# Top-k attention with an MLP on one core: values of the first 14 units half a step later, reciprocals one round later, three hurried pairs instead of five, eight pairs of q and k on chip instead of five

## The chip, the core and the metric

The kernel runs on one core of a Trainium2 chip. Its time is device microseconds (us), the median of several runs. One further execution was taken with the hardware profiler on; the views of the profile below come from that one.

## What is computed

Attention with a top-32 mask over 8 x 8 heads of 576 positions and 64 dimensions, and then a two-layer MLP with a leaky ReLU over the 4608 tokens:

```
scores = scale * q @ k^T                   # per head, 576 x 576
kth    = 32nd largest score of each row
scores = where(scores >= kth, scores, -1e9)
attn   = exp(scores - max); attn /= (sum(attn) + 1e-9)
x      = (attn @ v), heads side by side    # 4608 x 512
out    = leaky(x @ w_in) @ w_out           # 512 -> 2048 -> 512, slope 0.01
```

## The kernel before, in words

**Units and steps.** Two heads make a pair (32 pairs; four pairs are one batch element). A *unit* is 128 query rows of both heads of a pair, or the last 64 rows of two pairs. There are 144 units, 18 for each batch element. The main loop has one *step* s for each unit, and step s works on four units at once: the top-k of unit s, the mask and the exponents of unit s-1, the normalizing and the transposing of unit s-2, and the scores of units s+2 and s+3 (in even steps).

**What a unit passes through.** Scores: TensorE (PE) multiplies q and k into PSUM (L210), ScalarE (ACT) copies them to SBUF (L217). Top-k: VectorE (DVE) finds 32 maxima in four *rounds* of eight (L240, L245, L248). Mask: GpSimd (POOL; L258, L259). Exponents with row sums: ACT (L262), then `ze`, the sums plus 1e-9 (L267). Reciprocal of `ze`: DVE (L271). Normalizing: ACT (L274). Transposing: ACT splits the 32-bit weights into two 16-bit halves (L283), two DMAs write them to DRAM (`apart`, L284), and a DMA transpose reads them back as `wT` (L286), all DMAs issued in program order by SyncE (SP). Values: PE multiplies `wT` with v (`weigh_values`, L323), and ACT copies the product into x (`keep_values`, L337). When the four pairs of 128 or 256 tokens have their x, the MLP of this *chunk* can start.

**Hurried pairs.** An odd unit n in `HURRIED` (L425) is transposed by PE (L296) and copied by ACT (L302) instead of going through DRAM, and the values of units n-1 and n are then due one step sooner. `values_at` (L427) says in which step values are due; before, they are placed at the end of that step.

**Order of the work.** The order is written out by hand in the loop over s; every engine keeps it. A step has seven calls of `mlp_steps` between the four DVE rounds; each puts a share of MLP work into PE's order. The share is `EARLY_SHARE` (530) while chunk 2 is not yet ready; afterwards `slot_budget` spreads what is ready evenly up to the step in which the next chunk becomes ready. Chunks 0 and 1 have 128 tokens (units 0 to 3 and 4 to 7), all later ones 256; chunk 2 is units 8 to 15.

**Buffers.** `LOADED` = 5 pairs of q and k are in SBUF at a time. `load_more` (called at the end of each step) loads pair p when the scores of the last unit of pair p-5 are issued. The pool `raws` holds the weights as they arrive from DRAM (three tiles of 8 KB in each partition, tag `raw`); they are used only while the weights are rounded, ahead of the main loop. Further: five buffers `s_sb`, three `wT`, two `split`, in PSUM two `wide` and one `narrow`.

Of the kernel before, what the change touches and what calls it, by code (L numbers as in the profile page):

```python
# [8 lines left out]
F32 = mybir.dt.float32  # L9
U32 = mybir.dt.uint32  # L10
U16 = mybir.dt.uint16
# [8 lines left out]
def kernel(  # L20
# [14 lines left out]
    NPAIR, P, S = qT.shape  # L35
# [14 lines left out]
    WCH = 1024  # L50
# [5 lines left out]
    LOADED, LOADED_V = 5, 5  # L56
# [3 lines left out]
    loads = ctx.enter_context(tc.tile_pool(name="loads", bufs=LOADED))  # L60
    raws = ctx.enter_context(tc.tile_pool(name="raws", bufs=3))
# [33 lines left out]
    def load_weights(n):  # L95
        if n >= NPIECE:
            return
        if not AS_WORDS:
            nc.sync.dma_start(piece(n), weights[n])
            return  # L100
        raw_of[n] = raws.tile([P, WCH, 4], U16, name="raw")
        nc.sync.dma_start(raw_of[n].rearrange("p n w -> p (n w)"), weights[n])
# [50 lines left out]
    qk_of, v_of = {}, {}  # L153

    def load_qk(pi):
        qt = loads.tile([P, S], F32, name="qt")
        kt = loads.tile([P, S], F32, name="kt")
        nc.sync.dma_start(qt, qT[pi])
        nc.sync.dma_start(kt, kT[pi])
        qk_of[pi] = qt, kt  # L160

    def load_v(pi):
        v_of[pi] = loads.tile([P, NKC, 2, D], F32, name="vt", bufs=LOADED_V)
        nc.sync.dma_start(v_of[pi], vk[pi])
# [104 lines left out]
    def reciprocals(u):  # L269
        u.rz = small.tile([P, 2], F32, name="rz")  # L270
        nc.vector.reciprocal(u.rz, u.ze)  # L271

    def normalize(u, i):
        nc.scalar.activation(u.s[i], u.s[i], AF.Copy, bias=0.0, scale=u.rz[:, i:i + 1])  # L274
# [33 lines left out]
    def x_at(token):  # L308

        c = 0  # L310
        while token >= CHUNKS[c]:
            token -= CHUNKS[c]
            c += 1
        return c, token
# [47 lines left out]
    def mlp(ch):  # L362

        n = CHUNKS[ch]
        t0 = sum(CHUNKS[:ch])
        x = x_of[ch]
        if ch < EARLY:
            yield from hidden_of_few(x)
        for f0 in range(0, NFC if ch >= EARLY else 0, 2):
            ph = ps_ml.tile([P, 2, CHMAX], F32, name="ph", tag="ml")  # L370
            for i in range(2):
                f = f0 + i
                for c in range(HP):
                    nc.tensor.matmul(  # L374
                        ph[:, i, 0:n], w_in[c][:, f * P:(f + 1) * P], x[c][:, 0:n],
                        start=(c == 0), stop=(c == HP - 1),
                    )
                    if c == 1 or i == 0 and c == HP - 1:
                        yield 2 * max(n, 225)
            nc.scalar.activation(gT[:, f0:f0 + 2, 0:n], ph[:, :, 0:n], AF.Prelu, alpha=SLOPE)  # L380
            yield 2 * max(n, 225)
        for r0 in range(0, n, P):
            m = min(P, n - r0)
            pz = ps_ml.tile([P, 512], F32, name="pz", tag="ml")
            for f in range(NFC):
                nc.tensor.matmul(  # L386
                    pz[0:m, 0:DMODEL], gT[:, f, r0:r0 + m], w_out[f // 4][:, f % 4, :],
                    start=(f == 0), stop=(f == NFC - 1),
                )
                if f % 2 and f + 1 < NFC:  # L390
                    yield 2 * DMODEL
            o_sb = work.tile([P, DMODEL], F32, name="o_sb", bufs=1)
            nc.scalar.copy(o_sb[0:m], pz[0:m, 0:DMODEL])
            nc.sync.dma_start(out[t0 + r0:t0 + r0 + m, :], o_sb[0:m])
            yield 2 * DMODEL

    def mlp_cost(ch):
        n = CHUNKS[ch]
        if ch < EARLY:
            return NFC * DMODEL + NFC // 4 * (HP * 512 + 2 * P)  # L400
        return NFC * HP * max(n, 225) + -(-n // P) * NFC * DMODEL
# [4 lines left out]
    def mlp_steps(budget):  # L406
        owed[0] += budget
        while owed[0] > 0:
            if running[0] is None:
                if not ready:  # L410
                    owed[0] = 0.0
                    return
                running[0] = mlp(ready.pop(0))
            cost = next(running[0], None)
            if cost is None:
                running[0] = None
            else:
                owed[0] -= cost
                backlog[0] -= cost
# [2 lines left out]

    LAG = 3
    HURRY = 20
    HURRIED = {3, 7, 15, 23, 31}  # L425

    def values_at(n):  # L427

        return n + LAG + (n + LAG) % 2 - ((n | 1) in HURRIED)

    steps = units

# [3 lines left out]
    done_tokens, ready_at = [0] * len(CHUNKS), []  # L436
    for n, u in enumerate(steps):
        ch, _ = x_at(u.b * S + u.q0)
# [2 lines left out]
            ready_at.append((values_at(n), ch))  # L441
    assert [ch for _, ch in ready_at] == list(range(len(CHUNKS)))

    def attended(s):
        for at, ch in ready_at:
            if at == s:
                ready.append(ch)
                backlog[0] += mlp_cost(ch)

    def slot_budget(s):  # L450

        after = [at for at, _ in ready_at if at >= s]
        until = after[0] if after else s
        if len(after) >= len(CHUNKS) - EARLY:
            return EARLY_SHARE
        return backlog[0] / ((until + 1 - s) * SLOTS)

    EARLY_SHARE = 530
    SLOTS = 7

    with tc.manual_schedule():
        last = {p: n for n, u in enumerate(steps) for p in u.pairs}

        def load_more(s):

            for of, load, n, lag in ((qk_of, load_qk, LOADED, -2), (v_of, load_v, LOADED_V, LAG + 1)):
                while len(of) < NPAIR and (len(of) < n or last[len(of) - n] + lag <= s):
                    load(len(of))


        for n in range(3):
            load_weights(n)
        rounding = {}
        for n in range(NPIECE + 2):
            for i in (n, n - 1, n - 2) if AS_WORDS else ():
                if 0 <= i < NPIECE:
                    if i == n:
                        rounding[i] = round_weights(i)
                    next(rounding[i], None)
            load_weights(n + 3)  # L480
            if 6 <= n < 6 + HP:
                load_qk(n - 6)
            elif n == NPIECE - 3:
                first_scores(steps[0])
            elif n == NPIECE:
                first_scores(steps[1])
            if n == NPIECE - 1:
                load_v(0)
                load_v(1)

        def values(s):
            due = [u for n, u in enumerate(steps) if values_at(n) == s]
            if due:
                po = ps_sc.tile([P, 2, 512], F32, name="wide", bufs=2)[:, 0, 0:2 * P]
                po = po.rearrange("p (u n) -> p u n", u=2)
            else:
                return
            for part in (weigh_values, keep_values):
                for n, u in enumerate(due):
                    part(u, po[:, n, :])  # L500
            attended(s)

        for s in range(len(steps) + LAG + 1):
            cur, old, older, new = unit(s), unit(s - 1), unit(s - 2), ()
            if s % 2 == 0:
                new = [u for u in steps[s + 2:s + 4] if u]
            picks = top_k(cur) if cur else iter(())
            budget = slot_budget(s)

            def slot():  # L510
                next(picks, None)

            slot()
            if old:
                mask(old, 0)
                mask(old, 1)
            if older:
                reciprocals(older)
                normalize(older, 0)
                normalize(older, 1)  # L520
            mlp_steps(budget)
            slot()
            if s - 2 in HURRIED:
                transpose_in_haste(older)
            mlp_steps(budget)
            if old:
                exponents(old, 0)
            if older:
                keep_transposed(older) if s - 2 in HURRIED else transpose(older)
            slot()  # L530
            mlp_steps(budget)
            mlp_steps(budget)
            slot()
            mlp_steps(budget)
            if old:
                exponents(old, 1)
                sums(old)
            if new and s < HURRY:
                scores(new)
            values(s)  # L540
            if new and s >= HURRY:
                scores(new)
            budget = slot_budget(s + 1)
            mlp_steps(budget)
            mlp_steps(budget)
            load_more(s)
        mlp_steps(1e9)

# [57 lines left out]
```

## Time and profile before

| | |
|---|---|
| median of 4 runs | 1491.6 us (1489.47 to 1492.33) |
| the profiled execution, its own time | 1488.68 us |
| span from its first to its last instruction | 1486.9 us |
| PE busy | 1397.9 us (94%) |
| DVE busy | 1328.6 us (89%) |
| ACT busy | 1094.7 us (74%) |
| POOL busy | 1096.1 us (74%) |
| mean granted PE clock | 0.980 |

How to read it: the span begins with the rounding of the weights (to about 68 us), then the 144 steps follow, and after about 1400 us only the MLP of the last chunks is left. "PEclk" in a table of windows is the granted clock of TensorE as a share of full speed. In a timeline a line gives start, duration, engine, line of the kernel, operation, tiles and count, and in brackets the idle time of the engine ahead of it with what ended it. One fp32 matmul of the program shows as two in the profile.

### The profile page before, as it was taken

Reading aid. Unit: us, or ns where it says so; the run is one execution under the profiler, and the core shown is the slowest. Engines: PE = TensorE matmul, PEld = TensorE weight load, DVE = VectorE, ACT = ScalarE, POOL = GpSimd, SP = SyncE. Lnnn points to the kernel's source line nnn. Section 1 sums busy time; section 2 is a strip of 40 time slices with the busy share of each in tenths; the row PEclk is TensorE's granted clock in tenths of the full one; section 3 lists DMA queues with packets and bytes.
Section 4 is the critical chain, followed back from the end, with each engine's and each line's share of the span. In section 5 each row is a group of like instructions: output and inputs, shape, how many; then the busy total and the mean of one; then the engine's idle time right before and its main releaser. Section 6 shows DMA issues by size and latency. Waiting matters only on the chain.

```text
span 1486.9 us, 24127 instructions
## 1 busy us (share of the span) xinstructions
PE 1397.9 (94%) x8077; PEld 930.4 (63%) x8077; DVE 1328.6 (89%) x3414; ACT 1094.7 (74%) x1979; POOL 1096.1 (74%) x742
## 2 busy tenths in 40 slices
PE   6718978999999999999999999999999999999998
PEld 2305546676766767676766676767676767676674
DVE  7999998999999999999999999999999999999600
ACT  8657786777787777877777777787777777877720
POOL 2288887888788887788887888888888887788700
PEclk9958998999999999999999999999999999999999
DMA  8623354636566466646664566555665564645510
GB/s 329 246 71 90 96 168 118 176 103 160 148 173 152 130 176 157 177 130 172 164 173 128 142 172 162 164 143 159 174 164 142 135 171 140 169 128 142 144 46 14
DMA packets 386172, 221.12 MB, mean 149 GB/s; under 512 B 331520, under 2 KB 331520, under 8 KB 384000
## 3 DMA queue, kind: packets, MB, share of 16 engines
q1 hardware_dynamic: 386048, 219.59, 52.6%
q8 instruction: 63, 1.03, 0.3%
q14 instruction: 61, 0.50, 0.1%
HBM read 46.14 MB, written 91.42 MB: 93 GB/s over the span
## 4 chain that ended last, share of the span: by engine, by line
PE 84%; DVE 6%; ACT 4%; DMA 4%; issue 1%; SPq 0%; POOL 0%; DVEq 0%; ACTq 0%
PE pz L386 34%; PE ph L374 28%; PE wide L323 11%; PE wide L210 6%; PE narrow L210 3%; DMA wT<-apart 2%; ACT split L283 2%; DMA apart<-split 1%; DVE tops L245 1%; ACT s_sb L274 1%; ACT s_sb L262 1%; DVE pairs L248 1%; PE ph L348 1%; DVE w_out L149 1%; DVE w_in L149 1%
## 5 line engine op out<-in xcount | busy, mean ns | idle before, releaser
L258 POOL TENSOR_SCALAR pen<-s_sb,tops 128x576 f32<-128x576 f32 x288 | 637.5, 2213 | 222.7 <-DVE tops L245 131.7
L245 DVE MAX8 tops<-pairs 128x8 f32<-128x288 f32 (+1 forms) x1152 | 636.1, 592 | 0.0
L386 PE MATMUL pz<-w_out,gT 128*128 128x512 f32 x1152 | 508.3, 596 | 1.4 <-ACT gT L359 1.4
L374 PE MATMUL ph<-x,w_in 128*128 128x256 f32 x2176 | 481.1, 381 | 0.0
L248 DVE MATCH_REPLACE8 pairs<-tops,pairs 128x288 f32<-128x288 f32 (+1 forms) x864 | 460.3, 538 | 0.0
L374 PEld LDWEIGHTS ph<-x,w_in 128*128 128x128 f32 x2176 | 410.7, 190 | 77.1 <-issue 22.9
L259 POOL TENSOR_TENSOR s_sb<-s_sb,pen 128x576 f32<-128x576 f32 x288 | 406.2, 1411 | 24.1
L386 PEld LDWEIGHTS pz<-w_out,gT 128*128 128x128 f32 x1152 | 215.3, 190 | 266.2 <-issue 263.4
L283 ACT COPY split<-s_sb 128x1152 uint16<-128x1152 uint16 x278 | 304.8, 1145 | 0.0
L262 ACT ACTIVATE s_sb<-s_sb,nbias 128x576 f32<-128x576 f32 x288 | 221.1, 768 | 12.4 <-POOL s_sb L259 12.4
L274 ACT ACTIVATE s_sb<-s_sb,rz 128x576 f32<-128x576 f32 x288 | 207.1, 770 | 26.0 <-DVE rz L271 26.0
L240 DVE TENSOR_TENSOR pairs<-s_sb 128x576 f32<-128x576 f32 x288 | 213.4, 779 | 9.9
L323 PEld LDWEIGHTS wide<-wT,vt 128*64 128x64 f32 x3200 | 162.3, 140 | 65.7 <-issue 18.8
L323 PE MATMUL wide<-wT,vt 128*64 128x128 f32 (+1 forms) x3200 | 180.6, 269 | 22.8 <-ACT s_sb L217 14.5
L210 PE MATMUL wide<-kt,qt 64*128 64x352 f32 (+1 forms) x632 | 118.6, 490 | 27.3 <-ACT s_sb L217 22.0
L337 ACT COPY x<-wide 128x128 f32<-128x128 f32 (+1 forms) x160 | 32.2, 261 | 150.4 <-PE wide L323 150.3
L380 ACT ACTIVATE gT<-ph 128x512 f32<-128x512 f32 x136 | 80.6, 593 | 78.9 <-PE ph L374 78.9
L217 ACT COPY s_sb<-wide 128x704 f32<-128x704 f32 x142 | 107.1, 754 | 21.7 <-PE wide L210 21.7
L210 PE MATMUL narrow<-kt,qt 64*128 64x224 f32 (+1 forms) x632 | 69.2, 359 | 8.5 <-DMA kt<-in_kT_dram 8.5
L210 PEld LDWEIGHTS wide<-kt,qt 64*128 64x128 f32 (+1 forms) x632 | 48.5, 178 | 44.6 <-ACT s_sb L217 22.5
L271 DVE RECIPROCAL rz<-ze 128x2 f32<-128x2 f32 x144 | 22.4, 156 | 58.1 <-ACT ze L267 57.9
L217 ACT COPY s_sb<-narrow 128x448 f32<-128x448 f32 x142 | 68.7, 536 | 6.4 <-PE narrow L210 5.7
(58 smaller groups left out, 546.7 us busy)
## 6 DMA issues: line engine op xcount, KB each, us to landing
apart<-split SPq DMA_DIRECT2D x278, 288.0 KB, 2.1
raw<-in_weights_dram SPq DMA_DIRECT2D x16, 1024.0 KB, 7.0
vt<-in_vk_dram SPq DMA_DIRECT2D x32, 320.0 KB, 3.4
qt<-in_qT_dram SPq DMA_DIRECT2D x32, 288.0 KB, 3.6
kt<-in_kT_dram SPq DMA_DIRECT2D x32, 288.0 KB, 3.9
out_dram<-o_sb SPq DMA_DIRECT2D x36, 256.0 KB, 2.0
wT<-apart SPq DMA_TRANSPOSE x139, 4.6
```

The costliest lines, as they stand in the source:

```text
L210: nc.tensor.matmul(to[r0:r0 + u.rows, i, :], qt[d, u.q0:u.q0 + u.rows], kt[d, k0:k1], start=True, stop=True)
L240: nc.vector.tensor_tensor(pairs[:, :, n, :], u.both[:, :, 0:HS], u.both[:, :, HS:S], op)
L245: nc.vector.max(out=u.tops[:, i, r, :], in_=rest[i])
L248: nc.vector.match_replace(out=rest[i], in_to_replace=u.tops[:, i, r, :], in_values=rest[i], imm_value=LOWEST)
L258: nc.gpsimd.tensor_scalar(pen, u.s[i], u.tops[:, i, ROUNDS - 1, 7:8], MASKED, ALU.is_lt, ALU.mult)
L259: nc.gpsimd.tensor_tensor(u.s[i], u.s[i], pen, ALU.add)
L262: nc.scalar.activation(u.s[i], u.s[i], AF.Exp, bias=u.nbias[:, i:i + 1], scale=SCALE, accum_out=u.z[:, i:i + 1])
L274: nc.scalar.activation(u.s[i], u.s[i], AF.Copy, bias=0.0, scale=u.rz[:, i:i + 1])
L283: nc.scalar.copy(split, pairs[:, :, h])
L323: nc.tensor.matmul(po[side * D:(side + 1) * D, o, :], vt[:, c, side, :], u.wT[:, c + side * NKC if c + 1 < NKC else c, r:r + n], start=(c ...
L374: nc.tensor.matmul(ph[:, i, 0:n], w_in[c][:, f * P:(f + 1) * P], x[c][:, 0:n], start=(c == 0), stop=(c == HP - 1),)
L386: nc.tensor.matmul(pz[0:m, 0:DMODEL], gT[:, f, r0:r0 + m], w_out[f // 4][:, f % 4, :], start=(f == 0), stop=(f == NFC - 1),)
```

## The change

1. Values of units 0 to 13 are placed in the middle of step (n|1)+4, between the first and the second DVE round. Before, they stood at the end of step (n|1)+3, and for the pairs (2, 3) and (6, 7) at the end of step (n|1)+2. From unit 14 on nothing moves.
2. Units 3 and 7 are no longer hurried: their weights go through DRAM like the others.
3. In steps below 20, unless one of the units s-1 and s-2 is 15, the reciprocal and the normalizing of unit s-2 come after the second DVE round instead of the first.
4. Eight pairs of q and k are on chip. Of every eight pairs, the last three lie in the three `raw` tiles of the weights.
5. `EARLY_SHARE` is 500 instead of 530.

```diff
     def load_qk(pi):
-        qt = loads.tile([P, S], F32, name="qt")
-        kt = loads.tile([P, S], F32, name="kt")
+        if pi % (LOADED + 3) < LOADED:
+            qt = loads.tile([P, S], F32, name="qt")
+            kt = loads.tile([P, S], F32, name="kt")
+        else:
+            raw = raws.tile([P, WCH, 4], U16, name="raw").rearrange("p n w -> p (n w)").bitcast(F32)
+            qt, kt = raw[:, 0:S], raw[:, S:2 * S]
...
-    HURRIED = {3, 7, 15, 23, 31}
+    HURRIED = (15, 23, 31)
+    UNHURRIED = 14
+    MIDDLE, END = 0, 1
 
     def values_at(n):
 
-        return n + LAG + (n + LAG) % 2 - ((n | 1) in HURRIED)
+        if n < UNHURRIED:
+            return (n | 1) + LAG + 1, MIDDLE
+        return (n | 1) + LAG - ((n | 1) in HURRIED), END
...
-    EARLY_SHARE = 530
+    EARLY_SHARE = 500
...
-            for of, load, n, lag in ((qk_of, load_qk, LOADED, -2), (v_of, load_v, LOADED_V, LAG + 1)):
+            for of, load, n, lag in ((qk_of, load_qk, LOADED + 3, -2), (v_of, load_v, LOADED_V, LAG + 1)):
...
+        def weights_of(u):
+            reciprocals(u)
+            normalize(u, 0)
+            normalize(u, 1)
...
             if old:
                 mask(old, 0)
                 mask(old, 1)
-            if older:
-                reciprocals(older)
-                normalize(older, 0)
-                normalize(older, 1)
+            late = s < HURRY and not {s - 1, s - 2} & set(HURRIED)
+            if older and not late:
+                weights_of(older)
             mlp_steps(budget)
+            values(s, MIDDLE)
             slot()
+            if older and late:
+                weights_of(older)
             if s - 2 in HURRIED:
                 transpose_in_haste(older)
...
             if new and s < HURRY:
                 scores(new)
-            values(s)
+            values(s, END)
```

More of the change, by code (lines that the diff above doesn't have):

```diff
@@ L442, with attended @@
     assert [ch for _, ch in ready_at] == list(range(len(CHUNKS)))
-    def attended(s):
+    def attended(*place):
         for at, ch in ready_at:
-            if at == s:
+            if at == place:
                 ready.append(ch)
@@ L450, in slot_budget @@
     def slot_budget(s):
-        after = [at for at, _ in ready_at if at >= s]
+        after = [at for (at, _), _ in ready_at if at >= s]
         until = after[0] if after else s
@@ L489, with values @@
                 load_v(1)
-        def values(s):
-            due = [u for n, u in enumerate(steps) if values_at(n) == s]
+        def weights_of(u):
+            reciprocals(u)
+            normalize(u, 0)
+            normalize(u, 1)
+        def values(*place):
+            due = [u for n, u in enumerate(steps) if values_at(n) == place]
             if due:
@@ L500, in values @@
                     part(u, po[:, n, :])
-            attended(s)
+            attended(*place)
         for s in range(len(steps) + LAG + 1):
```

## The prediction

> **What bounds the kernel now.** I first cut the span into stretches in the table of windows: from the start of chunk 0's MLP to that of chunk 2's, from there to the end of DVE's work, and the rest. Columns: window and length, then busy us and instructions of PE, PEld, DVE, ACT and POOL, then PEclk, DMA share, GB/s.
>
> ```profile
> 124.38:239.66 115.28, 95.21 (x548) 52.46 (x546) 106.99 (x281) 85.70 (x162) 93.71 (x64) 0.93 0.45 128
> 239.66:1400.00 1160.34, 1154.02 (x6927) 794.23 (x6926) 1109.15 (x2886) 910.61 (x1679) 935.40 (x626) 1.00 0.56 152
> 1400.00:1486.90 86.90, 83.16 (x326) 50.52 (x324) 0.51 (x3) 18.32 (x33) 6.95 (x4) 0.99 0.18 53
> ```
>
> From 239.66 us on PE is busy 1237.2 of 1247.2 us at full clock: it sets the end. Before that it lacks work, since MLP work exists only once values are done. In the built order of the changed kernel, PE's 3635 instructions from chunk 2's first matmul to the end are those of before, in the same order. So the question is one number: when does chunk 2's MLP begin? Next, what PE waits for ahead of it (waits, 60 to 260 us: total us, times, longest):
>
> ```profile
> PE wide L210 <- ACT s_sb L217: 22.0, 1, 22.0
> PE wide L323 <- ACT s_sb L217: 14.5, 2, 13.5
> PE narrow L210 <- DMA kt<-in_kT_dram: 8.5, 1, 8.5
> PE wide L210 <- DMA kt<-in_kT_dram: 4.7, 1, 4.7
> ```
>
> The first two lie at 75 to 118 us, where there is no MLP work yet. The kt waits are the scores of units 18 and 19, whose pairs 5 to 7 are loaded only in steps 14 and 15. The chain that ended last shows that they are on the path:
>
> ```profile
> 212.01 1.44 ACT s_sb L274 x2
> 213.45 0.76 ACT s_sb L262 x2
> 214.21 2.10 ACT split L283 x2
> 216.33 3.31 DMA apart<-split
> ...
> 219.72 2.55 SPq L286
> ...
> 222.93 4.76 DMA kt<-in_kT_dram
> ...
> 230.02 3.71 PE wide L323 x40
> ...
> 237.33 2.40 PE wide L323 x40
> ```
>
> SP issues kt behind a transpose that waits for its halves. Then the values of units 12 and 13 (230.02) run at half clock, ACT's copies of them hold up the normalizing of unit 15, and only at 237.33 come the values of 14 and 15. Last, the timeline of PE, to see where chunk 0 begins:
>
> ```profile
> 112.73 4.32 PE L323 MATMUL wide<-wT,vt 128*64 128x128 f32 x40 [13.51 <-ACT s_sb L217]
> 118.26 1.43 PE L296 MATMUL wide<-ident,s_sb 128*128 128x128 f32 x9 [1.21 <-ACT s_sb L274]
> 120.68 3.77 PE L323 MATMUL wide<-wT,vt 128*64 128x128 f32 x40 [0.99 <-ACT wT L302]
> 124.38 7.13 PE L348 MATMUL ph<-w_in,x 128*128 128x512 f32 x16
> ```
>
> DVE sets the pace here: its step 0 starts at 68.34 and steps 1 to 7 follow every 8.84 us. Call t(s) the start of step s. Undisturbed, t(17) = 68.34 + 17 x 8.84 = 218.6; the timeline has 223.23. DVE's waits for `ze` make nearly all of the difference: 8.8 us in six up to 260 us, of which three (3.29, 1.06, 0.29) come after t(17), so 4.2 us before it.
>
> **Eight pairs.** Loads of pairs 5 to 7 (six of 288 KB, 0.43 to 0.70 us of SP each) move to step 0. They wait for the last readers of the weights' tiles (62.2 us), and the loads of v behind them land by some 68 us. Cover: SP's next instruction is at 92.29, DMA's share from 60 to 90 us is 0.03. Cost nothing; were the cover gone, 1.77 MB at the 385 GB/s of the window 45 to 60 us would cost 4.6 us. Both kt waits go (13.2 us of PE idle), but not 13.2 us of time: what is late next decides. Pairs 8 to 11 load in steps 14 and 15 instead, on the same queue, so the traffic ahead of the `wT` of units 13 and 14 stays.
>
> **No hurry for units 3 and 7.** PE loses 1.43 and 1.15 us, ACT swaps a 1.18 us copy for two splits of 2.19 (+1.0 us each, in steps where it has 1 to 3 us of waits), SP gets 2 x (1.4 + 2.55) us, in a queue idle more than half of the time here. The real price is that chunk 0 begins later. The values of units 2 and 3 now stand in PE's order behind the scores of 8 and 9. They need a `wide` buffer, which ACT frees at the end of step 6: reciprocal of unit 4 at t(6) + 4.6 = 126.0, normalizing 1.4, exponents 0.8, splits 2.1, exponents and `ze` 1.2, first copy 0.75: 132.5. At the cold price of the row above (4.32) they end at 136.8: chunk 0 begins 12.4 us later.
>
> **Does PE still finish chunks 0 and 1 in time?** It was busy 95.2 us from 124.38 to 239.66. Less scores of 8 and 9 (2.3, now ahead), one hurried unit (1.15) and what the cold clock added in the kt stall (scores 5.4 instead of 2.1, values 3.75 instead of 2.40, transposes 1.43 instead of 1.15; 5.0): 86.8 us. Idle: the short waits for ACT in that stretch (4.7) and the two about unit 15 (2.2). 136.8 + 86.8 + 6.9 = 230.5. The share of 500 gives 35 calls for each chunk of 17408; 70 calls from the middle of step 7 end with the first of step 17, just before chunk 2's values. So PE goes from waiting to nearly full.
>
> **Reciprocals a round later.** No instruction is added. The wait for `ze` gets 1.6 us more slack (a round): of 1.18, 2.83 and 0.2 us would remain 1.2. Against that, `keep_values` now stands on ACT ahead of normalizing, exponents, splits and `ze` in steps 5, 7, ... 17, and if PE is late there, all of these are, and then DVE. The trace of before shows this arrangement at step ends only. Lower bound of DVE's loss before t(17): 0; upper bound: 3.3 us (the longest wait here) in each second step from 8 to 16 less 1.6, 5 x 1.7 = 8.5. I take 2.2, nearer to the three waits of before less the slack.
>
> **When chunk 2 begins, by the chain.** Unit 13 is late: reciprocal t(15) + 4.6, splits end 4.4 later (rows 217.39 to 221.77), apart 2.1, transpose issued from t(15) + 11.2 to 13.8, that is t(16) + 4.9. Behind it four loads, 2.0: t(16) + 6.9. Unit 14's halves follow at once (its splits end at t(16) + 7.4) and take 6.3 us behind those loads (224.41 to 230.68), so its transpose is issued near t(17) + 4.6 and lands 4.6 later, t(17) + 9.2. Values 2.4: t(17) + 11.6. Unit 15 is ready sooner: reciprocal t(17) + 3.0, normalizing, copies, transposes and their copy give t(17) + 7.2. So `wT` of 14 is late next, and chunk 2 begins at 218.6 + 2.2 + 11.6 = 232.4, later than PE's own 230.5. Against 239.66: 7.2 us sooner.
>
> Two rules of the Trainium skill change this sum. "DMA: Bandwidth & Descriptors" (Where 436 GB/s comes from) puts about 358 GB/s on a core's HBM traffic: the 1.77 MB of four loads and two halves would take 4.9 us by that (an estimate) instead of 6.3, and chunk 2 would begin at 231.0. The trace has the very transfers, so 6.3 stays. "TensorE: Matmul & The Clock Gate" (HAM oscillation) speaks against the change: an idle gap beyond about 3.4 us halves the clock. The row 222 to 230 us agrees (PEclk 0.50). After unit 15's transposes (near t(17) + 6) PE waits for `wT` of 14 some 3 us. By the rule, were the gap a little longer, the values would take 4.8, not 2.4, and 2.4 us of gain would go; by the row of the cold values 1.35. I take the warm price and keep 2.4 for the range.
>
> **After chunk 2's start.** DVE has less lead over PE then (it began chunk 2 at t(18) + 7.5, now at t(18) + 2.7), while steps 18 and 19 also hold back their reciprocals. PE's waits for `wT` after 240 us are 6.3 us in six; I give back 1 us (0 to 3). Net -6.2. For the profiled execution 1488.7 - 6.2 = 1482.5; the runs' median lies 2.9 higher, so 1485.4.
>
> **The rivals.** *Larger gain*: DVE loses nothing and the loads don't hold up unit 14; then unit 15's transposes set chunk 2 at t(17) + 9.6 = 228.2, gain 11.4: 1480.2. For it: unit 14's halves need not queue if SP gets to the loads sooner. Against: PE's own 230.5. *No change*: PE is full from step 7, ACT's copies wait for it, DVE loses the 8.5; chunk 2 at 238.7, gain 1: 1490.6. For it: after 240 us, where PE is full, DVE waits 50.4 us for `ze` although nothing else holds it. *Slower*: the three `wT` buffers. With values of units 4 and 5 in the middle of step 9, `wT` of unit 4 is freed in the very step in which unit 7's transpose needs it, and SP, which keeps its order, holds halves and loads behind it; unit 7 then delays the values of 6 and 7, and so on. It decides once PE reaches the values later than t(s) + 12.5, where the transpose could be issued. PE begins at t(7) + 2.4, so it would have to slip 10 us. Price: one landing of 4.6 us as PE idle for three odd units, 13.8: chunk 2 at 246.2, 6.5 later, 1498.1.
>
> **How the numbers follow.** Main case 0.64, larger gain 0.13, no change 0.15, slower 0.08. A measurement can tell about 0.2% (3 us), so faster means below 1488.6. Main case: DVE's loss from 0 to 5, the cold 2.4, the 0 to 3 given back: 1482 to 1489. Faster 0.76, same 0.16, slower 0.08. The range reaches into the larger gain and to the edge of no change: 1480.5 to 1490.
>
> **What would show it.** Right: no wait for kt; chunk 0's first matmul near 137; t(17) near 221; chunk 2 near 232; `wT` of unit 14 released last before it; PE's stretch from there to the end as long as before (1247 us, +1). Wrong: DVE waits for `ze` above 5 us before t(17), SP waits at L286 for PE, or a longer stretch after chunk 2's start.

## The result and the profile after

The changed kernel takes 1487.59 us (median of 44 runs, 1483.52 to 1491.02), before 1490.32 us (63 runs, 1487.64 to 1494.37). The ratio is 0.9981, 95% interval 0.9976 to 0.9985: 2.7 us faster, less than half of the forecast 6.2. The profiled execution of the changed kernel took 1490.49 us (span 1488.7), 2.9 above the median; two more profiles of it follow below.

The table of windows of the changed kernel, cut at the same three events (chunk 0's first matmul, chunk 2's, the end of VectorE's work):

```profile
136.89:243.58 106.69, 93.58 (x524) 50.80 (x522) 98.14 (x256) 78.89 (x149) 83.12 (x57) 0.93 0.49 138
243.58:1403.00 1159.42, 1156.19 (x6930) 795.40 (x6929) 1106.00 (x2878) 911.44 (x1682) 936.58 (x626) 1.00 0.56 151
1403.00:1488.70 85.70, 81.94 (x323) 49.95 (x321) 0.33 (x2) 17.13 (x30) 5.75 (x4) 1.00 0.17 50
```

Chunk 0 begins at 136.89, as worked out (136.8). Chunk 2 begins at 243.58: not 7 us sooner than the 239.66 of before, but 3.9 us later. What PE waits for, 60 to 260 us:

```profile
PE wide L327 <- ACT s_sb L221: 25.7, 2, 13.9
PE wide L214 <- ACT s_sb L221: 23.6, 1, 23.6
PE wide L327 <- DMA wT<-apart: 6.3, 1, 6.3
PE pt L362 <- ACT scale L357: 4.9, 2, 2.9
```

The kt waits (13.2 us) are gone. The first row is 13.9 us ahead of the values of units 0 and 1, much as before (13.5), and 11.9 us, which are new, ahead of those of units 2 and 3. New too are the 6.3 us for transposed weights, and most of the 4.9 us for copies of ScalarE. The chain that ended last shows what now leads to chunk 2:

```profile
213.41 2.36 PE wide L327 x40
...
215.79 0.04 ACT x L341
...
216.22 1.33 ACT s_sb L278 x2
217.56 0.75 ACT s_sb L266 x2
218.31 2.09 ACT split L287 x2
220.40 0.78 ACT s_sb L266 x2
...
221.20 0.21 ACT ze L271
...
221.44 0.18 DVE rz L275
...
223.84 2.10 ACT split L287 x2
...
229.92 4.32 DMA apart<-split
...
234.32 4.66 DMA wT<-apart
...
239.11 4.54 PE wide L327 x40
```

The chain no longer runs over kt. The part shown starts at the values of units 10 and 11 on PE (213.41): ACT copies them, and only then normalizes unit 13, takes unit 14's exponents and its `ze`; for that DVE waits 5.04 us at its reciprocal; then come unit 14's splits, its halves and its transpose. The timeline of SP shows what lies between the end of the splits (225.94) and the transpose:

```profile
225.13 0.58 SPq L162 DMA_DIRECT2D qt<-in_qT_dram  x1
225.75 0.43 SPq L163 DMA_DIRECT2D kt<-in_kT_dram  x1
226.23 0.43 SPq L162 DMA_DIRECT2D qt<-in_qT_dram  x1
226.70 2.69 SPq L163 DMA_DIRECT2D kt<-in_kT_dram  x1
229.49 0.86 SPq L288 DMA_DIRECT2D apart<-split  x2
234.32 2.42 SPq L290 DMA_TRANSPOSE wT<-apart  x1
```

SP issues four loads ahead of unit 14's halves, and the last of them takes it 2.69 us instead of 0.43. The timeline of PE has the other end:

```profile
228.47 2.40 PE L327 MATMUL wide<-wT,vt 128*64 128x128 f32 x40
231.33 1.44 PE L300 MATMUL wide<-ident,s_sb 128*128 128x128 f32 x9 [0.46 <-ACT s_sb L278]
239.11 4.54 PE L327 MATMUL wide<-wT,vt 128*64 128x128 f32 x40 [6.34 <-DMA wT<-apart]
```

PE idles 6.34 us ahead of the values of units 14 and 15, and they then run at half clock, 4.54 us instead of 2.40.

### The profile page after: what moved, and what is told of

Its sections match the earlier page's. It is cut to its first block, busy times and chain, and to the rows that moved or that the text cites. A ratio compares the mean times of both kernels' runs of the same rounds, so it can differ in the third digit from the quotient of the medians.

```text
span 1488.7 us, 24084 instructions
## 1 busy us (share of the span) xinstructions
PE 1398.1 (94%) x8059; PEld 930.0 (62%) x8059; DVE 1328.5 (89%) x3414; ACT 1096.2 (74%) x1979; POOL 1096.1 (74%) x742
## 4 chain that ended last, share of the span: by engine, by line
PE 86%; DVE 7%; ACT 3%; DMA 3%; issue 1%; SPq 0%; POOL 0%; DVEq 0%; ACTq 0%
PE pz L390 32%; PE ph L378 31%; PE wide L327 11%; PE wide L214 6%; PE narrow L214 3%; DVE tops L249 2%; DVE pairs L252 1%; PE ph L352 1%; DMA wT<-apart 1%; ACT split L287 1%; DMA apart<-split 1%; DVE w_out L149 1%; ACT s_sb L278 1%; DVE w_in L149 1%; DVE scale L146 1%; ACT s_sb L266 1%
## 5 line engine op out<-in xcount | busy, mean ns | idle before, releaser
L287 ACT COPY split<-s_sb 128x1152 uint16<-128x1152 uint16 x282 | 309.1, 1144 | 0.0
L278 ACT ACTIVATE s_sb<-s_sb,rz 128x576 f32<-128x576 f32 x288 | 207.0, 769 | 34.0 <-DVE rz L275 34.0
L341 ACT COPY x<-wide 128x128 f32<-128x128 f32 (+1 forms) x160 | 32.1, 260 | 150.8 <-PE wide L327 150.7
L214 PE MATMUL wide<-kt,qt 64*128 64x352 f32 (+1 forms) x392 | 75.9, 502 | 24.3 <-ACT s_sb L221 23.6
L397 ACT COPY o_sb<-pz 128x512 f32<-128x512 f32 x36 | 21.1, 586 | 58.5 <-PE pz L390 58.5
L252 DVE MATCH_VALUE_LOAD pairs<-tops,pairs 128x8 f32 x864 | 62.6, 72 | 0.0
```

The lines of the kernel that those rows point to most:

```text
L214: nc.tensor.matmul(to[r0:r0 + u.rows, i, :], qt[d, u.q0:u.q0 + u.rows], kt[d, k0:k1], start=True, stop=True)
L252: nc.vector.match_replace(out=rest[i], in_to_replace=u.tops[:, i, r, :], in_values=rest[i], imm_value=LOWEST)
L287: nc.scalar.copy(split, pairs[:, :, h])
```

## The experiments

Times are medians; each ratio is to runs of the kernel before made beside them on the same chip, with the 95% interval. The medians of before differ from chip to chip (1490.0 to 1491.9 us), so kernels are compared by their ratios. To compare profiles I use two numbers: the start of chunk 2 counted from VectorE's first step, which itself moves between 68.3 and 69.7 us from run to run, and the time from there to the end of the span.

| kernel | median us | ratio, interval | chunk 2 from first step | rest | PE's waits for DMA in the rest |
|---|---|---|---|---|---|
| before, first profile | 1490.32 | | 171.3 | 1247.2 | 6.3 |
| before again (e5) | 1489.54 | 0.9992, 0.9979 to 1.0006 | 173.2 | 1244.9 | 4.2 |
| changed, first profile | 1487.59 | 0.9981, 0.9976 to 0.9985 | 174.9 | 1245.1 | 3.1 |
| changed again (e1) | 1487.85 | 0.9982, 0.9972 to 0.9991 | 174.6 | 1242.4 | 2.1 |
| changed, third profile (e12) | 1487.78 (one run) | | 171.6 | 1244.9 | 3.5 |
| eight pairs alone (e2) | 1490.08 | 0.9995, 0.9985 to 1.0004 | 173.8 | 1245.6 | 4.2 |
| changed, five pairs (e3) | 1491.40 | 1.0004, 0.9995 to 1.0013 | 175.1 | 1247.6 | 5.0 |
| changed, loads in steps 19, 20 (e4) | 1492.31 | 1.0012, 1.0003 to 1.0021 | 167.9 | 1254.1 | 10.2 |
| changed, loads spread (e6) | 1482.31 | 0.9948, 0.9935 to 0.9960 | 169.0 | 1241.5 | 1.9 |
| changed, early reciprocals (e7) | 1484.24 | 0.9955, 0.9940 to 0.9969 | 172.1 | 1241.7 | 2.1 |
| changed, share 530 (e8) | 1487.84 | 0.9990, 0.9980 to 1.0000 | 174.9 | 1245.0 | 3.4 |
| loads spread, early reciprocals (e9) | 1478.85 | 0.9913, 0.9899 to 0.9927 | 164.5 | 1244.9 | 4.5 |
| five pairs, early reciprocals (e10) | 1487.09 | 0.9968, 0.9958 to 0.9979 | 171.4 | 1245.6 | 4.2 |
| eight pairs alone, spread (e11) | 1485.52 | 0.9952, 0.9937 to 0.9967 | 168.3 | 1247.6 | 5.3 |

**Parts of the change.** Before I had a second profile, theory A was: everything after chunk 2's start is constant, its start is the time; the kt waits were on the path, and the loads of pairs 8 to 11 ahead of unit 14's halves took most of their place. Its rivals: eight pairs bring nothing, the later values do it alone; or unit 14 is late by its own splits.

Changed kernel, unaltered, for a second profile:

> The changed kernel once more, unaltered. In its profiled execution (1490.5 us, 2.9 above the median of its runs) VectorE lost 7.7 us to waits for ze ahead of step 17, and chunk 2 began at 243.6 us, later than in the profile of before (239.7). Theory A: the start of chunk 2 varies from run to run with VectorE's waits, and everything after it is constant (1245 to 1247 us): a run near the median, 1487.6, has chunk 2 near 240.5 and waits of 4 to 6 us. Rival: the start is fixed near 243.6 and the later part of the run varies; then chunk 2 begins at 243 to 244 again whatever the time.

The time came near the median (profiled execution 1487.76), but chunk 2 began at 243.59 again, as the rival has it. The 3 us between the two executions lie behind it: 1245.1 and 1242.4. So theory A fell: the rest is not constant.

Eight pairs and nothing else, put into the kernel before:

```diff
+        if pi % (LOADED + 3) < LOADED:
...
+        else:
+            raw = raws.tile([P, WCH, 4], U16, name="raw").rearrange("p n w -> p (n w)").bitcast(F32)
+            qt, kt = raw[:, 0:S], raw[:, S:2 * S]
...
-            for of, load, n, lag in ((qk_of, load_qk, LOADED, -2), (v_of, load_v, LOADED_V, LAG + 1)):
+            for of, load, n, lag in ((qk_of, load_qk, LOADED + 3, -2), (v_of, load_v, LOADED_V, LAG + 1)):
```

> Before, with eight pairs of q and k on chip and nothing else of the change. Theory A: the kt waits (13.2 us) go, but the values of units 14 and 15 then wait for the transposed weights of unit 14, whose halves still queue behind four loads (near 235.3 us in the profile of before), so chunk 2 begins at 237.5 to 239 and the time falls by 1 to 2 us, to 1488.3 to 1489.3. Rival B: the kt waits are the whole cost, chunk 2 begins near 232, and the time falls by 6 to 7 us. Rival C: the eight pairs bring nothing, the time stays at 1490.3.

1490.08, within the interval of no change. The kt waits are gone, and a wait of 5.1 us for unit 14's weights stands in their place, as theory A has it. But chunk 2 began at 243.47, not at 237.5 to 239, and the gain expected of it did not show: the time is that of rival C.

Changed kernel with five pairs:

```diff
-        if pi % (LOADED + 3) < LOADED:
-            qt = loads.tile([P, S], F32, name="qt")
-            kt = loads.tile([P, S], F32, name="kt")
-        else:
...
+        qt = loads.tile([P, S], F32, name="qt")
+        kt = loads.tile([P, S], F32, name="kt")
...
-            for of, load, n, lag in ((qk_of, load_qk, LOADED + 3, -2), (v_of, load_v, LOADED_V, LAG + 1)):
+            for of, load, n, lag in ((qk_of, load_qk, LOADED, -2), (v_of, load_v, LOADED_V, LAG + 1)):
```

> The changed kernel with five pairs of q and k on chip. Theory A: the scores of units 18 and 19 again wait for kt, now behind a TensorE that is later than before; chunk 2 begins at 244 to 248 and the time is 1491 to 1494, 3 to 7 us above the changed kernel. Rival C: the later values and reciprocals bring the gain by themselves, the time stays within 1 us of the changed kernel, near 1487.6.

1491.40, as theory A expected. So neither half of the change gains by itself: pairs alone -0.05%, the rest with five pairs +0.04%, both together -0.19%. The first two lie within the noise.

**The queue ahead of unit 14.** The loads of the changed kernel out of the way, first by five steps:

```diff
-            for of, load, n, lag in ((qk_of, load_qk, LOADED + 3, -2), (v_of, load_v, LOADED_V, LAG + 1)):
+            for of, load, n, lag in ((qk_of, load_qk, LOADED + 3, 3 if s < 22 else -2), (v_of, load_v, LOADED_V, LAG + 1)):
```

> The changed kernel with the loads of pairs 8 to 11 put into steps 19 and 20 instead of 14 and 15, behind the halves and transposes of units 13 and 14; they are first needed in step 34. Theory A: the weights of unit 14 land 3 to 5 us sooner, the gap before the values of 14 and 15 falls below 3 us and they run at full clock (2.4 us instead of 4.5); chunk 2 begins 5 to 7 us sooner and the time falls to 1481 to 1484. Rival: unit 14 is late by its own splits, which end at 225.8 in the profile of the changed kernel; then the halves need 2.1 us and the transpose 4.6 behind them and the time falls by 1 to 3 us only, to 1485 to 1486.5.

Chunk 2 began 6.1 us sooner (237.45) and PE's wait for unit 14 fell to 2.4 us, as theory A has it. But after this short wait the values of units 14 and 15 still ran at half clock, which theory A had ruled out, and the kernel became 4.5 us slower instead of faster. The timeline of PE shows both:

```profile
232.98 4.54 PE L327 MATMUL wide<-wT,vt 128*64 128x128 f32 x40 [2.42 <-DMA wT<-apart]
...
281.94 0.80 PE L327 MATMUL wide<-wT,vt 128*64 128x64 f32 x20 [1.01 <-DMA vt<-in_vk_dram]
288.68 2.69 PE L327 MATMUL wide<-wT,vt 128*64 128x64 f32 x40 [5.93 <-DMA wT<-apart]
```

The four loads now stand ahead of the halves of units 18 and 19, together with loads of v, and PE waits there (the last two lines). The queue was moved, not removed. Part of the 6.1 us need not be the edit's: the scores of units 16 and 17 ran at full clock here, as in the third profile of the changed kernel (below), and against that one chunk 2 is 3.7 us sooner. So the loads one at a time, in steps 23, 25, 27 and 29 (a table of least steps, looked up in `load_more`):

```diff
+    SPREAD = {8: 23, 9: 25, 10: 27, 11: 29}
...
+                    if of is qk_of and s < SPREAD.get(len(of), 0):
+                        break
```

> The changed kernel with the loads of pairs 8, 9, 10 and 11 at the ends of steps 23, 25, 27 and 29, one at a time (first needed in step 34). With them in steps 19 and 20 chunk 2 began 6.1 us sooner (237.5), but the values of the units behind waited 5.9 us for weights and 1.0 us for v at 280 to 289 us. Theory A with that correction: four loads in a row cost TensorE about 6 us wherever the weights of a unit queue behind them; one at a time they cost under 1 us each. Chunk 2 at 237 to 238.5, waits behind it 2 to 4 us, time 1480.5 to 1483.5. Rival: what is gained at chunk 2 is lost in any case, since VectorE needs its steps; time within 1 us of 1487.8.

1482.31, as expected; by the ratios 0.33%, some 5 us, below the changed kernel. SP and PE about unit 14:

```profile
225.33 1.29 SPq L288 DMA_DIRECT2D apart<-split  x2
230.94 2.52 SPq L290 DMA_TRANSPOSE wT<-apart  x1
```

```profile
235.71 2.40 PE L327 MATMUL wide<-wT,vt 128*64 128x128 f32 x40 [2.62 <-DMA wT<-apart]
```

The halves no longer stand behind loads, and PE waits 2.62 us for the weights instead of 6.0 to 6.3. The values then ran at full clock. So of the some 5.7 us by which chunk 2 is sooner, about 3.5 are the queue and 2.1 the clock, and the clock is not settled by the length of the gap: in e4 it fell after a shorter one. The halves were still not quick: 5.6 us from first issue to the transpose, against 3.5 in e9 below (222.01 to 225.50). In e6 most of the traffic had passed by 228.2 us and a remainder trickled at 16 to 32 GB/s until about 230.4; one 16 KB transfer of instructions (226.90 to 228.62 in the DMA records) lies just ahead of that. Whether it held the halves is not tested.

The same edit in the kernel before with eight pairs alone (the tiles of e2 and the table are left out here):

```diff
...
-            for of, load, n, lag in ((qk_of, load_qk, LOADED, -2), (v_of, load_v, LOADED_V, LAG + 1)):
+            for of, load, n, lag in ((qk_of, load_qk, LOADED + 3, -2), (v_of, load_v, LOADED_V, LAG + 1)):
...
+                    if of is qk_of and s < SPREAD.get(len(of), 0):
+                        break
```

> Before, with eight pairs on chip and the loads of pairs 8 to 11 spread over steps 23 to 29, nothing else of the change. With eight pairs alone the values of units 14 and 15 waited 5.1 us for transposed weights queued behind four loads, and the time fell by 0.3 to 0.7 us only. Theory A: without that queue chunk 2 begins 4 to 6 us sooner, near 238.5, and the time falls to 1484 to 1486.5. Rival: the weights of unit 14 are held by their splits, as values at the end of the step leave no room: within 1.5 us of eight pairs alone, 1488.5 to 1490.

1485.52: with the loads out of the way eight pairs do gain, 0.43% more than with the four loads in one place (e2).

**The reciprocals and the share.**

Before again, for a second profile:

> The kernel before, unaltered, for a second profile. In the profiles so far chunk 2 begins later in the changed kernel than before (243.6 against 239.7 us, 174.7 against 171.3 counted from VectorE's first step), and still the changed kernel is 2.8 us faster by its runs. Theory D: the gain lies after the start of chunk 2, where TensorE's waits for transposed weights are 6.3 us before and 2.1 to 2.7 in the two profiles of the changed kernel. Then this profile has chunk 2 at 171 to 173 from the first step again and waits of 6 to 9 us behind it. Rival: the first profile of before was a lucky one, and chunk 2 usually begins at 175 to 178; then it does so here.

Chunk 2 at 173.2 from the first step, just above the range of theory D; the waits behind it 4.2 us, below its range. So neither theory's range was met. Over two profiles of before and three of the changed kernel (e12 below) the waits behind chunk 2 are 5.3 and 2.9 us in the mean, which leans to theory D and does not settle it.

Reciprocals of the changed kernel back in their place:

```diff
-            late = s < HURRY and not {s - 1, s - 2} & set(HURRIED)
+            late = False
```

> The changed kernel with the reciprocals back behind the first round of VectorE in all steps. Theory A: each wait for ze ahead of step 17 grows by 1.6 us and some new ones appear, 4 to 8 us more in all, but the weights of each unit are ready 1.6 us sooner; chunk 2 begins 2 to 5 us later and the time is 1489 to 1492. Rival: ScalarE is held by TensorE in these steps whatever VectorE does, so the reciprocals change nothing: within 1 us of 1487.8.

Both expectations missed: the kernel became faster, by 0.26% in the ratios (some 4 us). The timelines of ACT in step 15 show why. First the changed kernel (second profile), then this one; L341 copies the values, L278 normalizes unit 13, L287 splits it:

```profile
216.14 0.43 ACT L341 COPY x<-wide 128x128 f32<-128x128 f32 x2 [5.22 <-PE wide L327]
216.46 1.45 ACT L278 ACTIVATE s_sb<-s_sb,rz 128x576 f32<-128x576 f32 x2
...
218.56 2.20 ACT L287 COPY split<-s_sb 128x1152 uint16<-128x1152 uint16 x2
```

```profile
209.40 1.44 ACT L278 ACTIVATE s_sb<-s_sb,rz 128x576 f32<-128x576 f32 x2
215.25 0.43 ACT L341 COPY x<-wide 128x128 f32<-128x128 f32 x2 [4.41 <-PE wide L327]
...
216.34 2.20 ACT L287 COPY split<-s_sb 128x1152 uint16<-128x1152 uint16 x2
```

`late` moves the normalizing not only behind a round of VectorE but also behind the copies of the values in ACT's order. There it stands still while ACT waits for PE; with the reciprocals early it is done in that time. The waits of ACT, 100 to 240 us, changed kernel and this one:

```profile
ACT x L341 <- PE wide L327: 17.5, 6, 5.2
ACT s_sb L278 <- DVE rz L275: 8.6, 6, 3.6
```

```profile
ACT s_sb L278 <- DVE rz L275: 13.8, 10, 3.6
ACT x L341 <- PE wide L327: 7.8, 6, 4.4
```

The waits for PE fall by 9.7 us, those for VectorE's reciprocals grow by 5.2. VectorE's loss ahead of step 17 falls from 7.8 to 5.9 us instead of growing, and chunk 0 begins at 135.07 instead of 137.20. The same edit on top of the changed kernel with five pairs (e3), so that the rest of the change is left without its reciprocals:

```diff
-            late = s < HURRY and not {s - 1, s - 2} & set(HURRIED)
+            late = False
```

> The changed kernel with five pairs of q and k and the reciprocals behind the first round: of the change only the later values, the hurried pairs and the share are left. Theory A: the scores of units 18 and 19 wait for kt again, and that wait lies on the path to chunk 2 whatever stands before it: 1487.5 to 1490, 3.5 to 6 us above the same kernel with eight pairs (1484.2). Rival: the later values gain 5 us by themselves and the pairs nothing, as they brought nothing alone: 1484 to 1485.5.

1487.09 lies between the two ranges, but before was slower on this chip (1491.88 us against 1490.0 for e7). By the ratios this kernel is 0.9968 and e7, with eight pairs, 0.9955, both with wide intervals: the pairs make 0.13% (some 2 us), which is not clear of the noise. So theory A's 3.5 to 6 us did not show, and the rival is nearer. The scores of units 18 and 19 still wait 3.3 us for kt. Later values, no hurry for units 3 and 7 and the share were not taken apart from each other.

Share of the changed kernel back at 530:

```diff
-    EARLY_SHARE = 500
+    EARLY_SHARE = 530
```

> The changed kernel with an early share of 530 instead of 500. Theory A: the MLP of chunks 0 and 1 is packed denser ahead of the values of units 4 to 11, TensorE reaches each of these later, ScalarE and then VectorE wait 1 to 3 us longer ahead of step 17, and chunk 2 begins that much later: 1488.5 to 1491. Rival: the share only moves idle time, since chunks 0 and 1 end ahead of step 17 either way: within 1 us of 1487.8.

1487.84, the rival: the share does nothing clear of the noise (ratio 0.9990, the changed kernel 0.9981, intervals overlapping).

**Both edits that gained**, the spread loads and the early reciprocals:

```diff
+    SPREAD = {8: 23, 9: 25, 10: 27, 11: 29}
...
-            late = s < HURRY and not {s - 1, s - 2} & set(HURRIED)
+            late = False
```

> The changed kernel with both edits that gained: the loads of pairs 8 to 11 one at a time in steps 23 to 29, and the reciprocals behind the first round in all steps. Theory A: they act at different places. Early reciprocals put the normalizing ahead of the copies of the values on ScalarE and bring unit 14 some 2 us sooner; spread loads take the queue from its halves. Chunk 2 at 234 to 236.5, against 240.9 and 238.0 with one of them, time 1478 to 1480.5. Rival: both remove the same wait for the weights of unit 14, so the second brings under 1 us: 1481.5 to 1483.

1478.85 us, ratio 0.9913 to before: the gains of the two edits (0.33% and 0.26% on the changed kernel's 0.19%) add up within the noise, so the rival is out. Chunk 2 began at 233.44, sooner than expected. PE's timeline there:

```profile
226.50 2.40 PE L327 MATMUL wide<-wT,vt 128*64 128x128 f32 x40
228.84 1.21 PE L300 MATMUL wide<-ident,s_sb 128*128 128x128 f32 x9
231.11 2.40 PE L327 MATMUL wide<-wT,vt 128*64 128x128 f32 x40 [1.07 <-ACT wT L306]
```

No wait for transposed weights is left ahead of chunk 2, and the clock stays full there (PEclk 1.00 from 212 to 233 us).

**A third profile of the changed kernel**, to see where its runs differ:

> The changed kernel a third time, for a third profile. Its 44 runs fall into groups by the mean granted clock: 1490.2 us at 0.977, 1488.0 at 0.978, 1485.9 at 0.979. Both profiles so far (0.977 and 0.978) show half clock in two places, the scores of units 16 and 17 (some 1.7 us) and the values of 14 and 15 (2.1 us). Theory E: the runs at 0.979 keep full clock in one or both, and begin chunk 2 2 to 4 us sooner, at 171 to 173 from VectorE's first step instead of 174.7; the part behind stays at 1241 us plus TensorE's waits. Rival: the start of chunk 2 is 174.7 in all runs and the later part holds the spread.

One run, 1487.78 us at a mean granted clock of 0.979. Chunk 2 at 241.11, 171.6 from the first step, as theory E expected: one of the two places kept full clock. The time is no lower than that of the second profile (1487.76), though, as the rest is 2.5 us longer. The scores of units 16 and 17, behind the same waits of 1.18 us (near 198) and 2.01 us, in the first profile and in this one:

```profile
205.92 1.23 PE L214 MATMUL wide<-kt,qt 64*64 64x352 f32 x8
206.91 1.74 PE L214 MATMUL narrow<-kt,qt 64*64 64x224 f32 x16
208.40 1.38 PE L214 MATMUL wide<-kt,qt 64*64 64x352 f32 x8
```

```profile
205.62 0.82 PE L214 MATMUL wide<-kt,qt 64*64 64x352 f32 x8
206.26 0.94 PE L214 MATMUL narrow<-kt,qt 64*64 64x224 f32 x16
207.01 0.77 PE L214 MATMUL wide<-kt,qt 64*64 64x352 f32 x8
```

3.8 us at about half clock (PEclk 0.79 from 204 to 212) against 2.1 us at full clock. The slower ones hold up the values of units 10 and 11 and with them everything in the chain above: VectorE's longest wait is 5.0 us in the first and 3.4 in this one.

## Why the prediction was right in sign and wrong in its steps

The kernel did become faster, and 1487.59 us lies within the stated range of 1480.5 to 1490. But the gain was to come from a chunk 2 that begins 7.2 us sooner, and the profiles do not show that: counted from VectorE's first step it begins at 171.6 to 174.9 us, before at 171.3 and 173.2. As far as the profiles tell, the right sign was luck.

- *Bound*: right. From chunk 2 on PE is full, and the rest is 1241 us plus PE's waits in it, within 1.6 us in every profile but e4's (1243.9), where part of it ran below full clock.
- *Eight pairs*: the kt waits went, and the loads of pairs 8 to 11 ahead of unit 14's halves were late next, as said. This step held best: with the loads spread the kernel is 0.33% faster, some 5 us (e6 against the changed kernel). With them in place pairs alone gave nothing (e2). The halves behind them took 6.8 us in e12 (issued at 225.02, transposed from 231.78), near the 6.3 taken from the trace of before; the estimate of 4.9 us was too short.
- *No hurry for units 3 and 7*: chunk 0 at 136.89 for 136.8, though the terms as printed add up to 132.25, not 132.5, ahead of the values. PE did finish chunks 0 and 1 in time.
- *Reciprocals a round later*: the step that failed. "No instruction is added" and the wait "gets 1.6 us more slack" priced them at a small gain. By the ratios they cost 0.36% with five pairs (e3 against e10) and 0.26% with eight (changed against e7), 4 to 5 us. I had named the cause, `keep_values` ahead of the normalizing, and bounded VectorE's loss at 0 and 8.5 us; I took 2.2, and the three profiles have 7.7, 7.8 and 4.9. A wait for `ze` above 5 us ahead of step 17 was the prediction's own sign of being wrong, and in two of the three it came. I had not seen that the reciprocal's place decides whether the normalizing stands ahead of those copies, so the edit that was to relieve the wait made it longer.
- *When chunk 2 begins*: t(17) + 11.6 was 220.8 + 11.6. Measured, in the first profile, 227.3 + 16.3: VectorE lost 5.5 us more than the 2.2 taken, its first step was 0.4 later, and 0.6 are left over; unit 14's weights came at t(17) + 11.7 instead of 9.2, and the values took 4.54.
- *The clock*: the Trainium skill's rule on gaps beyond about 3.4 us ("TensorE: Matmul & The Clock Gate", HAM oscillation), which I had weighed and not taken, gave the price in the changed kernel: the gap was 6.3 us, the values took 4.54 us against the 4.8 estimated from it. As a threshold it did not hold: after 2.62 us (e6) the values took 2.40, after 2.42 us (e4) they took 4.54.
- *After chunk 2*: I gave back 1 us for a smaller lead. PE's waits for DMA there became shorter: 3.1, 2.1 and 3.5 us against 6.3 and 4.2.
- *Rivals*: the mechanism of "no change" is near what happened (ACT's copies wait for PE, which is busy 93.6 of 106.7 us between the two chunks, and VectorE loses up to 7.8 of the 8.5 us); it had put the gain at 1 us. The wait for the third `wT` buffer was not seen as the end of any stall on this path.

Where the 2.7 us come from is only partly settled. The parts are: later values without hurry, with early reciprocals and five pairs, -0.32% (e10); eight pairs on top of that, -0.13% (e7), within the noise; late reciprocals, +0.26%; together the -0.19% of the whole. But by the profiles chunk 2 begins no sooner in the changed kernel, as said above, and the shorter waits behind it make 2.4 us of the means of three and two profiles. Runs of one kernel differ by more than that, so which of the later waits the change removes, and why, stays open.

## What to carry to other kernels

When a step is moved in a hand-written order, write out what it now stands behind on each engine: here an edit meant to give a reciprocal slack put the next ScalarE step behind a copy that waits for TensorE, and cost some 4 us. A prefetch that is made earlier must also be put where its successors' traffic meets no short deadline; here four loads in one place made TensorE wait some 3.5 us longer at chunk 2, or 5.9 us further on, and one at a time brought the whole kernel some 5 us. And when runs of one kernel spread over several us, one profile of each is not enough to say where a difference of 3 us lies.

## What the runs showed of the hardware

- The granted clock of PE can fall after short gaps, and the same gap does not always do it. In the first two profiles of the changed kernel the scores of units 16 and 17 ran at about half clock after waits of 1.18 and 2.01 us within 8 us; in the third, with the same waits, they ran at full clock. The same 40 matmuls took 4.54 us behind a gap of 2.42 us (e4) and 2.40 us behind one of 2.62 us (e6).
- Two halves of 288 KB, issued behind four loads of 288 KB each, took 6.3 us from first issue to the transpose in before (224.41 to 230.68) and 6.8 us in e12 (225.02 to 231.78); with the loads out of the way 5.6 us (e6) and 3.5 us (e9).
- The changed kernel's runs order by the mean granted clock: 1490.2 us at 0.977 (7 runs), 1488.0 at 0.978 (22), 1485.9 at 0.979 (14), and one at 0.980 with 1483.5. The profile e12, 1487.8 at 0.979, shows that the order holds for means only.
